# Where three turns of a weight conversion stand, and which scores go first, at the change from attention alone to attention beside dense products

## The chip, the cores and the metric

The kernel runs on one core of one Trainium2 chip. The metric is the device time of one execution in microseconds (us). Five engines work side by side, each through its own list of instructions in order: PE (matrix products; PEld is its weight load), DVE, ACT, POOL, and SP, which issues the DMAs.

## The reference

Attention with normalised queries and keys for 8 sequences, 12 heads, 448 positions, 64 wide, and then a SwiGLU block over the 8 x 448 = 3584 rows of 768. Inputs are float32, the three weight matrices arrive as float64.

```python
q_n, k_n = rmsnorm(q, g_q), rmsnorm(k, g_k)
scores = matmul(q_n, k_n^T) / sqrt(64)
attn = exp(scores - max) / (sum(exp(scores - max)) + 1e-9)
x = matmul(attn, v)                      # (8, 12, 448, 64) -> (3584, 768)
xn = x / sqrt(mean(x * x) + 1e-6) * rms_g
g, val = xn @ w_gate, xn @ w_val         # 768 -> 1536
out = (g * sigmoid(g) * val) @ w_out     # 1536 -> 768
```

## The kernel before

**Pairs of heads.** Attention is done two heads at a time: 48 pairs, six to a sequence, numbered g = 0 to 47. The main loop (L1276) has one block for each g. In block g the scores of pair g are made, pair g - 1 is finished, and pair g + 1 is transposed. The 448 key positions are three chunks of 128 and a remainder of 64, the "rest". The pieces of a block are these functions.

- `score(g, cs)`, L537: for each chunk in `cs` and both heads one product (L545) into a bank of `ps_s` (four banks), and an exponential on ACT (L549) into a tile `e`.
- `rests(g)`, L570: the rest's scores of pair g (L575, into a bank of `ps_s`); then, for pair g - 1, the first products of its output `av` (L581) and, for the first seven pairs, of its denominator `den` (L586); then the rest's exponential (L590). `av` lies in `ps_m`, a single bank, which is free again when pair g - 2's output has been read (L625).
- `values(g - 1)`, L592: the other products of `av` (L597). `sums(g - 1)`, L600: the other products of `den` (L610), the reciprocal on DVE (L614), and x = av * reciprocal on DVE (L625). Some steps later ACT squares x (L630) and POOL adds it to the sequence's sum of squares `ss` (L631).

**The bridge.** When a sequence's six pairs are done, `rms_x` (L640) sums `ss` over partitions by small products into `msx` (L645), DVE scales it (`ms`, L647), and POOL takes the power -1/2 (`rs`, L649). `norm_x` (L651) spreads `rs` over partitions by transposes into `rb` (L657), and six DVE instructions scale x by it (L663). Then the dense products can begin.

**The dense work** is cut into items that `fill` (L1155) puts between the pieces of the blocks. For sequence 0 they are, with numbers that are used below: items 0 to 47, gate and value products (L1122), item k using weight piece k; items 48 to 53, the first half of the output projection's columns for two row tiles of three parts each (L1004, four weight pieces of 48 to 59 each); items 54 to 59, the second half, with pieces 60 to 71. The first item comes in block 7, items 51 to 58 in block 13. From sequence 1 on, the weights are read back from DRAM, where the conversion stores them (`keep`, L772).

**The conversion** of the float64 weights to float32 is a pipeline in software. There are 72 pieces of 128 x 384, and `convert()` (L775) is one turn of it. Turn n issues the load of piece n on SP (L727), the *split* of piece n - 3 on ACT (two instructions, L740 and L741), the *join* of piece n - 4 on DVE (three, L746 to L748), the *add* of piece n - 5 on POOL (L785), and the store of piece n - 7 on SP (L773). There are 79 turns. The tile `top`, which a split writes and the add reads last, has four buffers (for some of the first 24 pieces three more of another pool). So the split of piece n waits for the add of piece n - 4.

Turns are issued at set places: 4 in block 0, 3 each in blocks 1 to 5, 3 at the end of block 6, which makes 22, and then one after every item. An item also carries the number of turns that must have been issued before it. Where that is not reached, `fill` issues the missing turns at once, one behind the other. For the output projection it is

```python
return [(NFC // OUT_PARTS * HALF, 4 * NFC + NFC * (n + 1) + 7, 0, ...)     # L1148
while turn_of["n"] < turns:                                                # L1166
    if not convert(): pe(idle)
pe(fn)
convert()
```

which gives 67 for items 48 to 53 and all 79 for items 54 to 59.

**Order.** Each engine's list follows the order in which the code issues. `pe(step)` counts one step on, runs it, and then runs what `after(n, ...)` has put n steps later.

Of the kernel before, what the change touches and what calls it, by code (L numbers as in the profile page):

```python
# [22 lines left out]
NPAIR = H // 2  # L23
# [312 lines left out]
def safe_scores(  # L336
# [42 lines left out]
    def after(n, fn):  # L379
        due.append((now["t"] + n, fn))  # L380

    def pe(fn):
        now["t"] += 1
        fn()
        for item in [d for d in due if d[0] <= now["t"]]:
            due.remove(item)
            item[1]()


    NG = B * NPAIR  # L390
# [4 lines left out]
    def own(j):  # L395
        return slice(j * D, (j + 1) * D)

    def across(j):
        return own(1 - j)
# [26 lines left out]
    def load_rests(b, i, engine):  # L426
        if b >= B:
            return
        if i == 0:
            st["rest", b] = rest_pool.tile([128, NPAIR, 2, D], F32, name="rest")  # L430
        for h in range(2):
            engine.dma_start(out=st["rest", b][own(i), :, 1 - h], in_=(q, k)[i][b, h::2, LAST].rearrange("h i d -> i h d"))

    def load_v_rests(b):
        if b >= B:
            return
        vr = st["vr", b] = rest_pool.tile([128, NPAIR, D], F32, name="vr")
        for h in range(2):
            nc.sync.dma_start(out=vr[across(h)], in_=v[b, h::2, LAST].rearrange("h i d -> i h d"))
# [31 lines left out]
    def direct(g):  # L471

        return g <= NPAIR
# [63 lines left out]
    def score(g, cs):  # L537

        qT, kT, rs = st["qT", g], st["kT", g], st["rs", g]
        sc = {}  # L540
        for c in cs:
            for j in range(2):
                r = across(j)
                ps = sc[c, j] = ps_s.tile([128, 512], F32, name="sc", tag="s")
                nc.tensor.matmul(ps[:, 0:S], lhsT=kT[r, c * 128:(c + 1) * 128], rhs=qT[r, :], start=True, stop=True)  # L545
        for (c, j), ps in sc.items():
            e = st["e", g, c, j] = e_pool.tile([128, S], F32, name="e")
            n = 2 * NK + c * 2 + 1 - j
            nc.scalar.activation(e, ps[:, 0:S], ACT.Exp, scale=rs[:, n:n + 1])  # L549


        def first():
            for j in range(2):
                es = st["es", g, j] = tmp.tile([128, S], F32, name="es", tag="es", bufs=4)
                nc.gpsimd.tensor_tensor(es, st["e", g, 0, j], st["e", g, 1, j], ALU.add)  # L555

        def more(of):
            for j in range(2):
                r = across(j) if of == "rest" else slice(0, 128)
                e = st["e", g, of] if of == "rest" else st["e", g, of, j]  # L560
                es = st["es", g, j]
                nc.gpsimd.tensor_tensor(es[r], es[r], e[r], ALU.add)  # L562

        if NK - 1 in cs and not direct(g):
            n = 3 if g == NPAIR + 1 else 2
            after(n, first)
            after(n + 2, lambda: more(2))
            after(n + 3, lambda: more("rest"))

    def rests(g):  # L570

        if g < NG:
            ps = ps_s.tile([128, 512], F32, name="sc", tag="s")
            for r in (own(0), own(1)):
                nc.tensor.matmul(ps[r, 0:S], lhsT=st["kT", g][r, LAST], rhs=st["qT", g][r, :], start=True, stop=True)  # L575
        if g:
            b, hp = divmod(g - 1, NPAIR)
            vr, e = st["vr", b][:, hp], st["e", g - 1, "rest"]
            av = st["av", g - 1] = ps_m.tile([128, 512], F32, name="av", tag="m")
            for j in range(2):  # L580
                nc.tensor.matmul(av[own(j), 0:S], lhsT=vr[across(j)], rhs=e[across(j)], start=True, stop=False,  # L581
                                 skip_group_check=True)
            if direct(g - 1):
                den = st["den", g - 1] = ps_f.tile([128, 512], F32, name="den", tag="f")
                for j in range(2):
                    nc.tensor.matmul(den[own(j), 0:S], lhsT=ones[across(j)], rhs=e[across(j)], start=True, stop=False,  # L586
                                     skip_group_check=True)
        if g < NG:
            e = st["e", g, "rest"] = e_pool.tile([128, S], F32, name="e")
            nc.scalar.activation(e, ps[:, 0:S], ACT.Exp)  # L590

    def values(g):  # L592

        vt, av = st["v", g], st["av", g]
        for c in range(NK):
            for j in range(2):
                nc.tensor.matmul(av[own(j), 0:S], lhsT=vt[:, j, c], rhs=st["e", g, c, j], start=False,  # L597
                                 stop=(c == NK - 1), skip_group_check=True)
# [41 lines left out]
    def rms_x(b):  # L640
        assert st["summed", b] == NPAIR - 1
        ss = st.pop(("ss", b))
        ps = (ps_s if b else ps_f).tile([128, 512], F32, name="msx", tag="s" if b else "f")
        for t in range(NT):
            nc.tensor.matmul(ps[0:P, t:t + 1], lhsT=ss[:, t * P:(t + 1) * P], rhs=ones[:, 0:1], start=True, stop=True)  # L645
        ms = small.tile([P, NT], F32, name="ms4")
        nc.vector.tensor_scalar(ms, ps[0:P, 0:NT], 1.0 / DM, 1e-6, ALU.mult, ALU.add)  # L647
        rs = st["rx", b] = small.tile([P, NT], F32, name="rs4")
        nc.gpsimd.tensor_tensor(rs, ms, mhalf[0:P, 0:NT], ALU.pow)  # L649
# [600 lines left out]
    def turns(n):  # L1250

        for _ in range(n):
            convert()
# [22 lines left out]
    for g in range(NG + 1):  # L1276
        b, hp = divmod(g, NPAIR)
        if g:
            load_pair(g + 3)
        if hp == 2:  # L1280
            for i in range(2):
                load_rests(b + 1, i, nc.sync)
            load_v_rests(b + 1)
        if g == 0:
            pe(lambda: score(0, (0,)))
            pe(lambda: rests(0))
            pe(lambda: score(0, (1,)))
            pe(lambda: turn(1, 0))
            pe(lambda: score(0, (2,)))
            norm_rests(0, 2, 4)  # L1290
            squares(2, 0)
            squares(2, 1)
            pe(lambda: turn(1, 1))
            for _ in range(3):
                convert()
            load_pair(3)
            load_v(2)
            convert()
            load_rows()
            continue  # L1300
        if g <= NPAIR:
            pe(lambda: score(g, (0,)))
            squares(g + 2, 0)
            squares(g + 2, 1)
            if g > 1:
                pe(lambda: turn(g + 1, 0))
                some_rests(g)
                pe(lambda: turn(g + 1, 1))
            pe(lambda: rests(g))
            pe(lambda: values(g - 1))  # L1310
            if g == 1:
                pe(lambda: turn(g + 1, 0))
                some_rests(g)
                pe(lambda: turn(g + 1, 1))
            load_v(g + 2)

            turns(1 if g == 1 else 3 if g < NPAIR else 0)
            pe(lambda: sums(g - 1))
            pe(lambda: score(g, (1, 2)))
            turns(2 if g == 1 else 3 if g == NPAIR else 0)  # L1320
            if g == 2:
                bound()
            continue

        pe(lambda: (rests(g), score(g, (0,)) if g < NG else None))
        if g == NPAIR + 1:
            pe(lambda: rms_x(0))
        pe(lambda: values(g - 1))
        load_v(g + 2)
        if g == NPAIR + 1:  # L1330
            pe(lambda: score(g, (1,)))
            pe(lambda: norm_x(0))
            pe(lambda: score(g, (2,)))
        pe(lambda: sums(g - 1))
        if g == NPAIR + 1:
            begin(0, 15)
        elif g < NG:
            pe(lambda: score(g, (1, 2)))
        st["block"] = now["t"]
        if hp:  # L1340
            fill()
            squares(g + 2, 0)
            squares(g + 2, 1)
            pe(lambda: turn(g + 1, 0))
            some_rests(g)
            fill()
            pe(lambda: turn(g + 1, 1))
            fill()
            continue
        fill(3)  # L1350
        pe(lambda: turn(g + 1, 0))
        fill(1)
        pe(lambda: rms_x(b - 1))
        squares(g + 2, 0)
        squares(g + 2, 1)
        pe(lambda: turn(g + 1, 1))
        fill(len(todo))
        begin(b - 1, 16)
        pe(lambda: norm_x(b - 1))
        fill()  # L1360
# [41 lines left out]
```

## Time and profile before

| | |
|---|---|
| median of 4 runs | 1597.73 us (1596.56 to 1598.63) |
| the profiled execution's own time | 1596.74 us |
| its span in the profile | 1595.0 us |
| PE busy | 1571.7 us, 99% |
| DVE busy | 872.3 us, 55% |
| ACT busy | 470.0 us, 29% |
| POOL busy | 658.7 us, 41% |

Times inside the execution count from the start of the span. The profiled execution's own time is its span and 1.74 us that lie around it. The shares of busy time are a mean over two unlike parts: up to about 280 us the weights are converted, and in most 20 us windows of that part DVE is busy for 15 to 19 us; afterwards DVE, ACT and POOL are busy about half of the time or less. PE is close to full in both.

### The profile page before, as it was taken

The page shows a single profiled execution, that of the slowest core. Times are in us where ns is not written, and L with a number is a line of the kernel's source. Part 1 is how long each engine was busy: PE and PEld are TensorE (multiplying, and loading weights), DVE is VectorE, ACT ScalarE, POOL GpSimd, SP SyncE. Part 2 cuts the span into 40 slices and gives each one's busy share as a digit, 9 for nine tenths or more (in the row PEclk, how much of TensorE's full clock was granted, in tenths as well). Part 3 has the DMA queues.
Part 4 walks back from the last instruction along what each step waited for, and adds up shares of the span by engine and source line. Part 5 has one row for each costly group of instructions (what it writes and reads, how often), then busy time and mean ns, then how long its engine had stood idle before and what let it go on. Part 6 is the DMA issues. An engine that isn't in the chain of part 4 may idle for free.

```text
span 1595.0 us, 21559 instructions
## 1 busy us (share of the span) xinstructions
PE 1571.7 (99%) x7286; PEld 1113.4 (70%) x7286; DVE 872.3 (55%) x1556; ACT 470.0 (29%) x940; POOL 658.7 (41%) x712
## 2 busy tenths in 40 slices
PE   8999999999999999999999999999999999999998
PEld 4344445687756887578865788667885688759974
DVE  6889898578822556236562354635563355613531
ACT  6746563232222222222232222323322222101010
POOL 6867877465334443344333443344542342000000
PEclk9999999999999999999999999999999999999999
DMA  7648574957746554465544655584554544457651
GB/s 210 206 151 257 162 251 124 289 187 243 250 141 204 156 154 121 141 205 155 154 119 142 205 154 148 149 266 132 160 146 124 176 141 139 120 176 214 174 154 52
DMA packets 261996, 273.28 MB, mean 171 GB/s; under 512 B 78836, under 2 KB 258804, under 8 KB 261876
## 3 DMA queue, kind: packets, MB, share of 16 engines
q1 hardware_dynamic: 260948, 271.61, 56.6%
q8 instruction: 60, 0.98, 0.3%
q14 instruction: 60, 0.49, 0.1%
q10 hardware_dynamic: 800, 0.20, 0.1%
q0 software_dynamic: 128, 0.00, 0.0%
HBM read 232.40 MB, written 39.32 MB: 170 GB/s over the span
## 4 chain that ended last, share of the span: by engine, by line
PE 78%; DVE 7%; issue 1%; DMA 0%; POOL 0%; SPq 0%; ACT 0%; DVEq 0%; POOLq 0%
PE ff L902 39%; PE ff L1094 22%; PE sc L545 6%; PE av L597 5%; PE sc L575 2%; PE den L610 2%; PE tr L527 1%; DVE top L747 1%; DVE top L748 1%; DVE top L746 1%; PE ff L1004 1%; DVE rd L618 1%; DVE h L925 0%; DVE h L924 0%; DVE ms L487 0%
## 5 line engine op out<-in xcount | busy, mean ns | idle before, releaser
L902 PE MATMUL ff<-x,w 128*128 128x224 f32 x1878 | 381.5, 354 | 0.1
L902 PEld LDWEIGHTS ff<-x,w 128*128 128x128 f32 x1878 | 351.3, 190 | 15.3 <-issue 11.7
L555 POOL TENSOR_TENSOR es<-e 128x448 f32<-128x448 f32 x82 | 91.5, 1137 | 493.0 <-ACT e L549 493.0
L902 PE MATMUL ff<-xs,w 128*128 128x224 f32 x1374 | 281.7, 353 | 4.5 <-DVE w L858 2.9
L902 PEld LDWEIGHTS ff<-xs,w 128*128 128x128 f32 x1374 | 258.0, 190 | 8.8 <-issue 6.0
L562 POOL TENSOR_TENSOR es<-es,e 64x448 f32<-64x448 f32 (+1 forms) x164 | 191.6, 1179 | 6.3
L618 DVE RECIPROCAL rd<-rd 128x448 f32<-128x448 f32 x41 | 121.0, 2952 | 113.5 <-ACT rd L617 113.5
L549 ACT ACTIVATE e<-sc,rs 128x448 f32<-128x448 f32 x288 | 161.2, 634 | 50.4 <-PE sc L545 48.0
L1094 PE MATMUL ff<-w,h 128*128 128x384 f32 x498 | 167.8, 487 | 0.6 <-ACT p L1073 0.6
L1094 PE MATMUL ff<-w,raw 128*128 128x384 f32 x468 | 159.6, 487 | 0.3 <-DVE y L1066 0.3
L545 PE MATMUL sc<-qT,kT 64*128 64x448 f32 x576 | 138.0, 572 | 1.9 <-ACT e L549 0.7
L1094 PEld LDWEIGHTS ff<-w,h 128*128 128x128 f32 x498 | 93.5, 190 | 64.5 <-issue 1.3
L1094 PEld LDWEIGHTS ff<-w,raw 128*128 128x128 f32 x468 | 87.6, 190 | 60.9 <-issue 2.6
L597 PE MATMUL av<-e,vt 128*64 128x448 f32 x576 | 118.8, 548 | 0.0
L506 POOL TENSOR_TENSOR rs<-ms,mhalf 128x12 f32<-128x12 f32 (+1 forms) x50 | 114.5, 2291 | 4.2
L1122 PE MATMUL ff<-x,w 128*128 128x448 f32 x288 | 111.8, 541 | 0.0
L545 PEld LDWEIGHTS sc<-qT,kT 64*128 64x128 f32 x576 | 53.9, 185 | 82.4 <-issue 68.5
L914 DVE TENSOR_TENSOR cc<-ff,u 128x448 f32<-128x448 f32 x84 | 52.3, 622 | 87.3 <-PE ff L902 87.2
L597 PEld LDWEIGHTS av<-e,vt 128*64 128x64 f32 x576 | 37.1, 136 | 75.6 <-issue 74.2
L1122 PEld LDWEIGHTS ff<-x,w 128*128 128x128 f32 x288 | 53.3, 190 | 50.8 <-issue 49.0
L631 POOL TENSOR_TENSOR ss<-ss,rd 128x448 f32<-128x448 f32 x40 | 46.5, 1163 | 82.9 <-ACT rd L630 82.9
L935 ACT COPY p<-ff 128x448 f32<-128x448 f32 x42 | 22.4, 532 | 192.6 <-PE ff L902 192.6
(132 smaller groups left out, 1858.3 us busy)
## 6 DMA issues: line engine op xcount, KB each, us to landing
w<-kept SPq DMA_DIRECT2D x511, 192.0 KB, 2.6
w<-kept_o SPq DMA_DIRECT2D x296, 192.0 KB, 2.8
kept<-w SPq DMA_DIRECT2D x89, 192.0 KB, 3.8
qk<-in_q_dram SPq DMA_DIRECT2D x48, 192.0 KB, 2.9
qk<-in_k_dram SPq DMA_DIRECT2D x96, 96.0 KB, 3.3
vt<-in_v_dram SPq DMA_DIRECT2D x48, 192.0 KB, 2.5
raw<-in_moe_w_gate_dram SPq DMA_DIRECT2D x24, 384.0 KB, 4.5
raw<-in_moe_w_val_dram SPq DMA_DIRECT2D x24, 384.0 KB, 4.6
```

The costliest lines, as they stand in the source:

```text
L506: nc.gpsimd.tensor_tensor(st["rs", g][:, cols], ms, mhalf[:, cols], ALU.pow)
L545: nc.tensor.matmul(ps[:, 0:S], lhsT=kT[r, c * 128:(c + 1) * 128], rhs=qT[r, :], start=True, stop=True)
L549: nc.scalar.activation(e, ps[:, 0:S], ACT.Exp, scale=rs[:, n:n + 1])
L555: nc.gpsimd.tensor_tensor(es, st["e", g, 0, j], st["e", g, 1, j], ALU.add)
L562: nc.gpsimd.tensor_tensor(es[r], es[r], e[r], ALU.add)
L597: nc.tensor.matmul(av[own(j), 0:S], lhsT=vt[:, j, c], rhs=st["e", g, c, j], start=False, stop=(c == NK - 1), skip_group_check=True)
L618: nc.vector.reciprocal(rd, rd)
L631: after(1 if soon else 4, lambda: (nc.gpsimd.tensor_tensor(ss, ss, rd, ALU.add), st.update({("summed", b): hp})))
L902: nc.tensor.matmul(bank[:, w * HT:(w + 1) * HT], lhsT=wt[:, c * 128:(c + 1) * 128], rhs=x[:, c, :], start=onto is None and w == c == 0, st ...
L914: nc.vector.tensor_tensor(add[name], ps[:, 0:S], add[other], ALU.add)
L1094: nc.tensor.matmul(ps, lhsT=left_o(b, which, LEFT_O[name], c), rhs=data(("wo", b, name, c)), start=first and c == 0, stop=c == NFP - 1, sk ...
L1122: nc.tensor.matmul(bank[w][:, 0:S], lhsT=data(key)[:, c * 128:(c + 1) * 128], rhs=st["x", 0, half][:, c, :], start=half == c == 0, stop=ha ...
```

## The change

In block 6, the last of the first sequence, the three turns of the conversion at the end of the block are left out; the count of 79 stays, so that they are issued later. In block 7 the scores of chunk 0 are issued ahead of `rests(7)`, and the two are separate steps of `pe`; before, `rests(7)` came first and both were one step. All other blocks go as they did.

```diff
             turns(1 if g == 1 else 3 if g < NPAIR else 0)
             pe(lambda: sums(g - 1))
             pe(lambda: score(g, (1, 2)))
-            turns(2 if g == 1 else 3 if g == NPAIR else 0)
+            turns(2 if g == 1 else 0)
             if g == 2:
                 bound()
             continue
 
-        pe(lambda: (rests(g), score(g, (0,)) if g < NG else None))
         if g == NPAIR + 1:
+            pe(lambda: score(g, (0,)))
+            pe(lambda: rests(g))
             pe(lambda: rms_x(0))
+        else:
+            pe(lambda: (rests(g), score(g, (0,)) if g < NG else None))
         pe(lambda: values(g - 1))
         load_v(g + 2)
         if g == NPAIR + 1:
```

## The prediction

> **What bounds the kernel now.** I read the page first, for the shares, then the waits of PE in the first 320 us, because block 7 and the whole conversion lie there, then the timeline at each wait, and last the chain of waits towards the place where the conversion ends.
>
> ```profile
> PE 1571.7 (99%) x7286; PEld 1113.4 (70%) x7286; DVE 872.3 (55%) x1556; ACT 470.0 (29%) x940; POOL 658.7 (41%) x712
> ```
>
> PE is idle for 23.3 us of the span. What the change can win is a part of that, and PE's waits name the part:
>
> ```profile
> PE av L581 <- issue: 1.2, 1, 1.2
> PE rb L657 <- POOL rs L649: 1.0, 1, 1.0
> ```
>
> Both lie between pair 6's last scores and the first dense product. PE's timeline, and DVE's below it:
>
> ```profile
> 83.82 0.97 PE L575 MATMUL sc<-qT,kT 64*64 64x448 f32 x4
> 85.98 0.97 PE L581 MATMUL av<-e,vr 64*64 64x448 f32 x4 [1.19 <-issue]
> 86.75 0.95 PE L586 MATMUL den<-e,ones 64*64 64x448 f32 x4
> 87.63 1.02 PE L545 MATMUL sc<-qT,kT 64*128 64x448 f32 x4
> 88.58 0.95 PE L645 MATMUL msx<-ones,ss 128*112 128x1 f32 x8
> 89.46 2.48 PE L597 MATMUL av<-e,vt 128*64 128x448 f32 x12
> 91.86 1.02 PE L545 MATMUL sc<-qT,kT 64*128 64x448 f32 x4
> 93.91 0.60 PE L657 MATMUL rb<-ident,rs 112*128 112x112 f32 x4 [1.02 <-POOL rs L649]
> ```
> ```profile
> 85.26 0.62 DVE L625 TENSOR_TENSOR x<-av,rd 128x448 f32<-128x448 f32 x1
> ...
> 92.13 0.56 DVE L748 SCALAR_TENSOR_TENSOR top<-raw,top 128x384 int32<-128x384 int32 x1
> 92.61 0.15 DVE L647 TENSOR_SCALAR ms<-msx 112x4 f32<-112x4 f32 x1
> ```
>
> The wait at 85.98 ends with pair 5's x (85.26 + 0.62 = 85.88), which frees the only `av` bank. The wait at 93.91 is the conversion's: `msx` is summed by 89.5, but `ms` stands on DVE behind three joins until 92.61, and `rs` and `rb` come after it. From 97.8 PE runs on the dense products. Where the conversion ends, the chain of waits runs through it:
>
> ```profile
> 272.49 0.93 DVE ms L487 x2
> ...
> 273.82 2.47 POOL rs L506
> ...
> 277.34 1.95 POOL w L785 x2
> 279.29 0.04 issue
> 279.34 3.82 PE ff L1004 x11
> ```
>
> The two adds are those of pieces 70 and 71. The products of 279.34 read piece 71, as the last pair of item 56. So the conversion arrives here just with PE: it has no room left at all.
>
> **The change, part by part.** All times are on the clock of before.
>
> *The scores first.* They take the place of the rests at 83.82 and fill the hole: two banks of `ps_s` come free with the exponentials that run from 83.13 at about 0.55 each. They take 0.95 (87.63 to 88.58), and the rests' 0.97 end at about 85.75. L581 still waits for x and starts at 85.98 as now; it and L586 take until 87.63. There `msx` is next, 0.95 earlier than now, if `ss` is ready. The square on ACT starts with x's end at 85.97 and takes 0.58; POOL's sum started at 86.63 and took 1.51, against 1.14 at 77.83. With no joins on DVE I take 1.14: ready at 87.8, `msx` at 87.85 instead of 88.58.
>
> *The turns gone from here.* Six ACT, nine DVE, three POOL instructions and three loads and three stores on SP leave. Behind them stood `ms` on DVE, `rs` on POOL, and on ACT and SP the rest's exponential and pair 10's loads, for which nobody waits. `ms` then follows `msx` at 88.9, `rs` takes 1.02 and is there at 90.1. PE has values and scores to do until 87.85 + (91.86 + 0.95 - 88.58) = 92.08, so `rb` starts at 92.08 without a wait, not at 93.91: **1.83 us won**. The six scalings (3.64) and the denominator behind `rb` keep their distances, so the dense items start 1.83 earlier, and so does the DVE work that waits for `rb`.
>
> *The turns come back.* After item k the turns issued are now 20 + k, not 23 + k. Items 0 to 47 need only piece k, for which 6 + k turns are enough (the code asks for 11 + k at most). Items 48 to 53 need 67, which 19 + 48 just reaches, and piece 59's add at item 45 (about 250 in the trace) is ahead of its use at about 256. Items 54 to 59 need 79: item 53 leaves 76 now and 73 after the change. So `fill` issues six turns in a row instead of three, in front of item 54. In those three of now only one add is left (piece 71); in the six there are four adds (68 to 71), three joins (69 to 71) and two splits (70, 71). The moved turns' three loads and stores spread over places where SP's loads come tens of us ahead; I cost them at nothing, and at some tenths if a load of a pair lands late.
>
> *What the burst costs.* On POOL the add after item 53 is at 277.30, behind pair 15's norm, whose place doesn't change; it is now piece 67's. The next adds follow about 0.97 apart (277.30 to 279.28 for two): 68 ready at 279.3, 69 at 280.3, 70 at 281.2. Piece 71 hangs on a longer thread: its split needs the `top` buffer that add 67 frees at 278.3; 0.56 on ACT gives 278.95; then its join on DVE. A join of now ends the DVE list in 1.33 alone and takes 2.96 beside adds:
>
> ```profile
> 224.21 0.57 DVE L746 TENSOR_SCALAR top<-top 128x384 f32<-128x384 f32 x1 [0.97 <-ACT top L740]
> 224.82 1.06 DVE L747 TENSOR_SCALAR top<-top 128x384 int32<-128x384 int32 x1
> 225.91 1.26 DVE L748 SCALAR_TENSOR_TENSOR top<-raw,top 128x384 int32<-128x384 int32 x1
> ```
> ```profile
> 222.26 4.50 POOL L785 TENSOR_TENSOR w<-top,raw 128x384 int32<-128x384 int32 x4
> ```
>
> It lies beside adds 68 to 70, so I take 2.96: joined at 281.95, added by 283.0. PE, which without waits would be at piece 67's use (item 55's last pair) at about 276.2 and at piece 71's at 279.1, stops at each piece in turn and reaches the last at 283.0 instead of 279.34: **3.66 us lost**. If the join took 1.33, the adds set the end at 282.2: 2.9 lost. If each of the five adds took 1.5 (the longest add in the trace took 1.507), they end at 284.8: 5.5 lost. Below 2.9 I find nothing: POOL has one add at a time.
>
> *Behind the burst.* The stores of the last pieces and the first weights of sequence 1 (279.67 on SP) stand behind the last add, and move with PE by the same amount, as do the differences on DVE that wait for those loads (284.49). The DVE waits of PE near 362 and 387 (1.4 and 1.5) follow the item order and stay.
>
> **The sum:** 1596.74 - 1.83 + 3.66 = 1598.6 for an execution like the profiled one. The median of the runs is 0.99 above it, so 1597.73 + 1.83 = **1599.6**. A measurement of this kernel can tell about 0.2%, 3.2 us, from no change.
>
> PE's clock matters where PE stops. The trace shows full clock (the 1.00 ahead of the DMA share) in the window that holds both waits of now:
>
> ```profile
> 80.00:100.00 20.00, 17.78 (x86) 6.96 (x83) 15.71 (x19) 10.16 (x20) 11.54 (x11) 1.00 0.69 213
> ```
>
> The longest single stop that I expect in the burst is 2.2 (276.2 to 278.4), twice the 1.19 that the trace shows at full clock, with other work on both sides; I take full clock.
>
> The Trainium skill (TensorE: Matmul & The Clock Gate, What's actually happening) says that an idle window of about 3.4 us halves PE's clock until a busy one of that length has passed. If the burst's stops did trip it, an estimate from that page adds 3.4 x (1 - 1/2) = 1.7 us and makes the sum 1601.3.
>
> **The rivals.** *The small loss* (the forecast): head won, burst lost, net 0 to +3.2. Own range 1597.8 to 1600.9. Chance 0.57.
>
> *The burst is free, or nearly:* only the head counts, 1595.9 with 1.83, down to 1594.9 if both waits go whole (1.19 + 1.02 on the profile's count, 2.8 with the modelled ends). For it: DVE was idle 2.20 before 277.32 and POOL 3.69 before 269.71, so the engines have time in sum. Against it: the adds stand behind pair 15's norm in POOL's list, and the idle time lies ahead of it. Faster by 3.2 would need the wait of 0.8 for `kT` near 241 to go as well. Chance 0.15, of which 0.06 is beyond 0.2%.
>
> *The burst costs more than 5.0:* PE's stop at item 56 grows past 3.2 + 1.83. One mechanism, the POOL adds in a row: it decides from about 1.4 us for each of five adds, which beside DVE joins some adds do take (1.33 to 1.5). At 1.5 the net is 5.5 - 1.83 = +3.7, 1601.4; if DVE's backlog (no wait of it from 225 to 275) also doesn't come 1.83 earlier, +5.5, 1603.2. Chance 0.28.
>
> *The change doesn't fill the hole at 85.98:* if pair 7's first scores wait for their banks, the first wait only changes its name, and the head wins 1.1 instead of 1.83. That shifts the forecast to 1600.3 and is inside it.
>
> **How the numbers follow.** Faster than 0.2%: 0.06. Slower than 0.2%: the third case, 0.28. The rest, 0.66, is within. The range leaves out the tail of the second case below 1595.5 and of the third above 1602.2.
>
> **What would show it.** In the changed profile: no wait before L581 above 0.3 and none before `rb`; the first L1122 at about 96.0; three adds (L785) fewer ahead of it; five adds in a row on POOL from about 275.5 to 281.2, with no other work of POOL between; PE waits on POOL L785 at L1004 of 3 to 4 us in sum, where PE had next to none before; from there all times 1.8 later than before. I am wrong if L1004 has no such wait, or if PE's new waits lie elsewhere.

## The result, and the profile after

Median 1600.77 us of 33 runs, against 1598.26 us of 53 runs of the kernel before. The ratio is 1.0015, 95% interval 1.0011 to 1.0020: some 2.4 us (1.8 to 3.2) slower, inside the 0.2% that a measurement of this kernel can tell from no change when it stands alone, and clear of zero with this many runs. The profiled execution took 1600.84 us, its span 1599.0 us.

Executions of all these kernels come in two groups about 1.6 us apart, which the first 12 us set; the profiled one of before is of the shorter group and that of after of the longer one, so below all steps are counted from pair 0's first scores (first L545, 10.81 before and 12.47 after). With this 1.66 taken off, the change shows two steps and nothing else:

| mark | before | after | difference, start taken off |
|---|---|---|---|
| first dense product (L1122) | 97.80 | 97.62 | -1.84 |
| first output product (L1004) | 248.77 | 248.57 | -1.86 |
| sequence 1's first product (L902) | 294.75 | 298.83 | +2.42 |
| end of the span | 1594.95 | 1599.05 | +2.44 |

**The head.** PE's timeline of after, from the rests to the first dense product, and DVE's beside it:

```profile
86.97 0.97 PE L575 MATMUL sc<-qT,kT 64*64 64x448 f32 x4
87.67 0.97 PE L581 MATMUL av<-e,vr 64*64 64x448 f32 x4
88.44 0.95 PE L586 MATMUL den<-e,ones 64*64 64x448 f32 x4
89.50 0.95 PE L645 MATMUL msx<-ones,ss 128*112 128x1 f32 x8
...
93.73 0.60 PE L657 MATMUL rb<-ident,rs 112*128 112x112 f32 x4
```
```profile
86.94 0.62 DVE L625 TENSOR_TENSOR x<-av,rd 128x448 f32<-128x448 f32 x1
90.48 0.16 DVE L647 TENSOR_SCALAR ms<-msx 112x4 f32<-112x4 f32 x1 [2.92 <-PE msx L645]
94.37 3.05 DVE L663 SCALAR_TENSOR_TENSOR x<-x,rg,rb 128x448 f32<-128x448 f32 x5 [3.72 <-PE rb L657]
```

Neither L581 nor L657 has a wait in brackets any more. DVE now waits 2.92 us for `msx`, where before the finished `msx` waited for DVE, and then 3.72 us for `rb`.

**The burst.** PE's waits between 262 and 300 us (there were none in this stretch before), POOL's and ACT's timeline there, and two windows of 5 us, in which the figure ahead of the DMA share is the granted clock:

```profile
PE ff L1004 <- POOL w L785: 2.6, 1, 2.6
```
```profile
276.13 1.26 POOL L511 TENSOR_TENSOR qn<-qk,rs 128x192 f32<-128x192 f32 x2
277.35 4.46 POOL L785 TENSOR_TENSOR w<-top,raw 128x384 int32<-128x384 int32 x4
282.36 1.00 POOL L785 TENSOR_TENSOR w<-top,raw 128x384 int32<-128x384 int32 x1 [0.55 <-issue]
```
```profile
278.70 0.55 ACT L740 ACTIVATE top<-raw 128x384 f32<-128x384 f32 x1 [6.71 <-POOL w L785]
```
```profile
275.00:280.00 5.00, 2.39 (x10) 1.32 (x9) 3.35 (x8) 1.03 (x2) 4.92 (x6) 1.00 0.33 117
280.00:285.00 5.00, 5.00 (x11) 2.18 (x10) 2.66 (x3) 0.48 (x1) 4.29 (x5) 0.66 0.49 169
```

Five adds stand in a row behind pair 15's norm, and the last split waits for the add of piece 67, as the prediction had it. What it had not: the granted clock falls to half from 280.0 to 283.4. This hardly costs anything here. Item 56's four weight pieces are taken up by PE at 279.80, 280.86, 282.22 and 283.48, and the adds that they need end at 279.65, 280.73, 281.81 and 283.36. The third piece is taken up 0.4 us behind its add, because products at half clock follow 0.64 us apart. The last is taken up 0.12 behind its add, just when the slow products ahead of it are through. So two limits end within 0.1 us of each other, the row of adds and the slow products, and the clock costs that 0.1 at most.

### The profile page after: what moved, and what is told of

The parts are those of the page before. It is cut to its first block, busy times and chain, and to the rows that moved or that the text cites. A ratio compares the mean times of both kernels' runs of the same rounds, so it can differ in the third digit from the quotient of the medians.

```text
span 1599.0 us, 21562 instructions
## 1 busy us (share of the span) xinstructions
PE 1575.5 (99%) x7286; PEld 1115.7 (70%) x7286; DVE 870.9 (54%) x1556; ACT 470.7 (29%) x940; POOL 660.2 (41%) x712
## 4 chain that ended last, share of the span: by engine, by line
PE 81%; DVE 6%; issue 0%; DMA 0%; POOL 0%; ACT 0%; DVEq 0%
PE ff L902 40%; PE ff L1094 22%; PE sc L545 6%; PE av L597 5%; PE sc L575 2%; PE den L610 2%; PE ff L1004 2%; PE tr L527 1%; DVE top L747 1%; DVE top L748 1%; DVE top L746 0%; PE ff L1122 0%; DVE h L925 0%; DVE h L924 0%; DVE rd L618 0%
## 5 line engine op out<-in xcount | busy, mean ns | idle before, releaser
L902 PE MATMUL ff<-x,w 128*128 128x224 f32 x1878 | 381.5, 354 | 0.1
L902 PEld LDWEIGHTS ff<-x,w 128*128 128x128 f32 x1878 | 351.3, 190 | 15.3 <-issue 11.1
L902 PE MATMUL ff<-xs,w 128*128 128x224 f32 x1374 | 281.7, 353 | 4.4 <-DVE w L858 2.9
L902 PEld LDWEIGHTS ff<-xs,w 128*128 128x128 f32 x1374 | 258.0, 190 | 8.6 <-issue 6.0
L545 PE MATMUL sc<-qT,kT 64*128 64x448 f32 x576 | 138.5, 572 | 1.9 <-ACT e L549 0.7
L545 PEld LDWEIGHTS sc<-qT,kT 64*128 64x128 f32 x576 | 54.2, 185 | 82.6 <-issue 69.2
L1122 PE MATMUL ff<-x,w 128*128 128x448 f32 x288 | 111.8, 541 | 0.0
L1122 PEld LDWEIGHTS ff<-x,w 128*128 128x128 f32 x288 | 53.3, 190 | 50.8 <-issue 49.0
L785 POOL TENSOR_TENSOR w<-top,raw 128x384 int32<-128x384 int32 x63 | 67.8, 1088 | 34.9 <-DVE top L748 25.7
L631 POOL TENSOR_TENSOR ss<-ss,rd 128x448 f32<-128x448 f32 x40 | 46.4, 1160 | 82.4 <-ACT rd L630 82.4
```

Of the source, the lines that this page charges most:

```text
L785: nc.gpsimd.tensor_tensor(data(key).bitcast(I32), top, lo, ALU.add)
L902: nc.tensor.matmul(bank[:, w * HT:(w + 1) * HT], lhsT=wt[:, c * 128:(c + 1) * 128], rhs=x[:, c, :], start=onto is None and w == c == 0, st ...
L1122: nc.tensor.matmul(bank[w][:, 0:S], lhsT=data(key)[:, c * 128:(c + 1) * 128], rhs=st["x", 0, half][:, c, :], start=half == c == 0, stop=ha ...
```

## The experiments

Twelve kernels that differ from before or after in a few words. The table gives what each did by its profile, in us against before with the start taken off, and the measured ratio to the kernel before. The stretches are bounded by the marks of the table above.

| run | to first dense product | to first output product | to sequence 1 | behind it | span | ratio (95% interval) |
|---|---|---|---|---|---|---|
| the change | -1.84 | -0.02 | +4.28 | +0.02 | +2.44 | 1.0015 (1.0011 to 1.0020) |
| e1, turns only | -1.03 | -0.01 | +4.31 | +0.08 | +3.35 | 1.0022 (1.0013 to 1.0032) |
| e2, order only | +0.03 | +0.04 | -0.01 | -0.17 | -0.10 | 1.0 (0.9991 to 1.0009) |
| e3, given back in block 7 | -1.83 | +6.43 | +0.02 | -0.17 | +4.45 | 1.0032 (1.0019 to 1.0044) |
| e4, norm later on POOL | -1.86 | -0.03 | +6.11 | +0.20 | +4.42 | 1.0022 (1.0013 to 1.0031) |
| e5, one turn kept | -1.43 | +0.01 | +2.46 | -0.07 | +0.98 | 1.0006 (0.9997 to 1.0015) |
| e6, two mid, one end | -1.46 | +0.06 | 0.00 | +0.01 | -1.40 | 0.9992 (0.9983 to 1.0001) |
| e7, three mid | -1.34 | +0.06 | 0.00 | +0.05 | -1.23 | 0.9992 (0.9983 to 1.0001) |
| e8, free top buffer | -1.81 | +0.04 | +4.30 | +0.08 | +2.61 | 1.0016 (1.0007 to 1.0025) |
| e9, three behind `ms` | -1.62 | +2.10 | -0.01 | -0.26 | +0.21 | 1.0003 (0.9994 to 1.0012) |
| e10, two mid, one behind `ms` | -1.85 | +0.02 | +0.01 | -0.10 | -1.91 | 0.9987 (0.9978 to 0.9996) |
| e11, two mid, one end, old order | -1.08 | +0.02 | -0.02 | -0.04 | -1.11 | 0.9995 (0.9986 to 1.0004) |
| e12, e4 with PE kept busy | -1.80 | +0.03 | +3.51 | +0.22 | +1.95 | 1.0012 (1.0003 to 1.0021) |

### The two halves of the change

e1 takes the turns out and keeps the old order:

```diff
-            turns(2 if g == 1 else 3 if g == NPAIR else 0)
+            turns(2 if g == 1 else 0)
```

> Only the three turns leave block 6; the rests stay ahead of the scores. My theory: the wait of av (L581) near 86 stays, the wait of rb (L657) goes, so the first dense product comes 1.1 us earlier than before; the burst in front of item 54 is that of the full change and costs 4.3 us. Sum +3.2 us against before, 0.8 us above the full change. Rival (the turns alone win the whole head): first dense product 1.85 us earlier, sum +2.4 us.

It did what the theory said: -1.03 and +4.31, sum +3.35. PE's wait for `av` is there as before:

```profile
88.01 0.97 PE L581 MATMUL av<-e,vr 64*64 64x448 f32 x4 [1.20 <-issue]
```

e2 is the change with `3 if g == NPAIR` put back in that line, so that only the order differs.

> Only the order of the first scores and the rests of pair 7 is changed; the three turns stay in block 6. My theory: the hole before av (L581) is filled, but ms (L647) still stands on DVE behind three joins, which end at 92.6 us whatever PE does, so rb (L657) starts at 93.9 as before and the wait of 1.0 us before it grows to about 1.7: 0 us against before, and no burst. Rival (each part is worth its own wait): first dense product 0.75 us earlier, sum -0.75 us.

The hole before `av` is gone and nothing is won; the time went into a wait of 0.49 us of `msx` for the sum of squares on POOL and into a longer wait for `rb` (1.41, before 1.02), since `ms` still stands on DVE behind the joins until 92.69:

```profile
94.00 0.60 PE L657 MATMUL rb<-ident,rs 112*128 112x112 f32 x4 [1.41 <-POOL rs L649]
```
```profile
92.22 0.56 DVE L748 SCALAR_TENSOR_TENSOR top<-raw,top 128x384 int32<-128x384 int32 x1
92.69 0.15 DVE L647 TENSOR_SCALAR ms<-msx 112x4 f32<-112x4 f32 x1
```

So the order alone is worth 0, the turns alone 1.03, both together 1.84. The burst belongs to the turns alone.

### Is it the missing three turns, and where else can they stand?

e3 gives the turns back in block 7, one behind each of its three groups of items (`fill()`), so that item 54 finds 76 turns as before.

```diff
+            more = 1 if g == NPAIR + 1 else 0
             fill()
+            turns(more)
             squares(g + 2, 0)
 ...
             fill()
+            turns(more)
             pe(lambda: turn(g + 1, 1))
             fill()
+            turns(more)
             continue
```

> The full change, and the three missing turns are issued in block 7, one after each of its three groups of dense items, so that 76 turns are out after item 53 again and the burst is three turns long as before. My theory (the loss is the longer burst alone): the head keeps its 1.85 us and the wait of L1004 on the add is back at 0.1 us: -1.85 us against before, 4.2 us below the full change. Rival (the conversion has no room between 98 and 277 us, so 60 turns there instead of 57 push its whole chain back): the adds of pieces 70 and 71 come 2 to 4 us later than before relative to PE and the sum is between 0 and +2 us.

The burst is gone (+0.02), which shows that it was the missing turns. But 6.43 us were lost at a new place, more than the rival had allowed, and not where the rival put it: between 105 and 130 us, not at the adds of pieces 70 and 71. PE's and ACT's waits and a window of that run:

```profile
PE sc L545 <- ACT e L590: 3.5, 1, 3.5
```
```profile
ACT top L740 <- DMA raw<-in_moe_w_gate_dram: 7.2, 1, 7.2
```
```profile
125.00:130.00 5.00, 4.08 (x9) 2.17 (x10) 4.90 (x6) 4.43 (x9) 3.10 (x4) 0.66 1.08 358
```

A split waits 7.2 us on ACT for its weight piece, and pair 8's exponentials stand behind it in ACT's list; PE stops 3.5 us for their banks, and then the granted clock is half for 3.4 us: the eight score products behind the stop took 3.79 us, against 1.77 for eight of the kind in the kernel before (L545 near 82). What held the load is not shown.

e9 puts all three behind `ms`, in the 3.7 us in which DVE waits for `rb`. The others put turns in the middle of block 6, ahead of `sums(5)`: e7 all three, e6 two with the third at the end of the block, e10 two with the third behind `ms`. e11 is e6 with the old order of scores and rests. The edits in short:

```diff
 # e9: turns(3); e10: turns(1)
             pe(lambda: rms_x(0))
+            turns(3)
 # middle of block 6: e6, e10, e11 two; e7 three
-            turns(1 if g == 1 else 3 if g < NPAIR else 0)
+            turns(1 if g == 1 else 3 if g < NPAIR else 2)
 # end of block 6: e6, e11 one
-            turns(2 if g == 1 else 0)
+            turns(2 if g == 1 else 1 if g == NPAIR else 0)
```

> The full change, with the three turns issued in block 7 right behind the step that makes msx, ms and rs, so that their joins stand behind ms on DVE instead of in front of it, where DVE waits 3.7 us for rb. No longer burst (22 turns before item 0). My theory: rb as early as in the full change (-1.8 us); three joins need 4.0 us alone, up to 6 beside adds, so the scalings of x start 0.3 to 2.3 us later than rb allows, of which PE has 2.6 us of other work to hide it; sum -1.4 to -1.85 us against before. Rival (DVE's list from 98 to 277 us has no room, so its later start comes back at the adds of pieces 70 and 71): L1004 waits 0.4 to 2.3 us on the adds near 277, sum -1.4 to +0.5 us.

The head was as expected (-1.62) and 2.10 us were lost later, but again earlier than the rival had it: PE waits 1.8 us for a copy of `kT` on DVE near 112 (two waits of the kind up to 320 us; before had one, of 0.8).

```profile
PE tr L527 <- DVE kT L533: 2.7, 2, 1.8
```

The joins ran beside POOL's `rs` and adds and took 6.6 us, the scalings began at 97.24 instead of 94.37, and DVE did not make it up in 12 us.

> The full change, and the three turns go back into block 6: two in its middle, ahead of the sums of pair 5, where DVE idles 3.3 us ahead of the reciprocal, and one at its end. 22 turns are out before item 0 as before, so no longer burst. My theory (the slots ahead of rb were the only free DVE time, so the turns must stay ahead of it, but not in front of ms): the joins end before the reciprocal (82.3), ms follows msx at once, head -1.5 to -1.85 us, burst 0: sum -1.5 to -1.85 us against before. Rival (turns in the middle hold an exponential on ACT or the reciprocal on DVE): the wait of av near 86 comes back with 1 to 2 us, sum 0 us or above.

> The same with all three turns in the middle of block 6. My theory: three joins need 4.0 us where DVE idles 3.3, the reciprocal comes 0.7 us late, and av (L581) waits about 0.85 us: sum -1.2 us against before. Rival as for two in the middle: sum 0 us or above.

By the profile they win 1.40 and 1.23 us: e7 as the theory said, e6 0.1 less than its range. The ratios agree, but their intervals end just above 1. The heads fall 0.4 to 0.5 us short of the change's. In e7 the reciprocal and with it `av` start 0.5 us later than in the change. In e6 the join at the end of block 6 stands beside the sum of squares on POOL, and `msx` waits for it; that sum (L631) takes 1.50 us there, and 1.13 in the change, where no join is beside it.

```profile
88.23 0.95 PE L645 MATMUL msx<-ones,ss 128*112 128x1 f32 x8 [0.48 <-POOL ss L631]
```

> Two turns in the middle of block 6 and one at its end, but the rests of pair 7 stay ahead of its first scores. My theory: the wait of av near 86 stays, ms is free, and rb comes 1.05 us earlier than before: sum -1.05 us, so that the order is worth 0.4 us more once the turns are out of the way (in the run with the order alone it was worth nothing). Rival (the order is worth nothing in any place of the turns): -1.47 us.

-1.08: with the turns out of the way the order is worth 0.38 us, as expected.

> The full change, with two of the three turns in the middle of block 6 and the third right behind the step of msx, ms and rs. My theory: no join stands beside the sum of squares on POOL or ahead of ms, so the head is the full change's -1.85 us and not the -1.47 us of two in the middle and one at the end of block 6; the one join behind ms ends 2 us before rb; burst as before: -1.85 us against before. Rival (a turn in block 7 holds ACT's exponentials as it did where three were given back): PE waits on an exponential in block 7, sum -1 us or above.

-1.85 in the head and nothing lost behind it. The one join behind `ms` took 2.7 us beside POOL's `rs` and an add, and still left DVE 1.08 us to wait for `rb`:

```profile
94.61 3.64 DVE L663 SCALAR_TENSOR_TENSOR x<-x,rg,rb 128x448 f32<-128x448 f32 x6 [1.08 <-PE rb L657]
```

This version is faster than both kernels: 0.9987 of before (0.9978 to 0.9996), some 2.1 us, and 0.9972 of after by the two ratios. Against before that too is inside 0.2%. Three turns that cost 4.3 us as a burst cost nothing where DVE has time that ends in a wait for PE.

### What sets the length of the burst

e5 keeps one of the three turns at the end of block 6 (`1 if g == NPAIR`), so that the burst has five.

> The full change with one of the three turns left at the end of block 6, so that the burst in front of item 54 is five turns. If the loss there is adds in a row behind pair 15's norm, with piece 71 held by its top buffer only when that buffer is freed by an add of the same row (which needs six turns), then the row is four adds (4.5 us from 277.4) and piece 71 is ready 1.5 us earlier than in the full change: loss 2.7 instead of 4.3 us. The head keeps 1.5 to 1.85 us (one join is done before ms needs DVE). Sum +1.0 us against before (+0.8 to +1.2). Rival (each moved turn costs the same): loss 2.9 us and a head of 1.2, sum +1.6 us.

+2.46 in place of 4.28, with four adds in the row and no split waiting for one of them; sum +0.98. The head, -1.43, is just short of its range.

```profile
277.89 4.21 POOL L785 TENSOR_TENSOR w<-top,raw 128x384 int32<-128x384 int32 x4
```

The clock stays at 1.00 in the profiled execution, with a single stop of 1.6 us. This fits the row of adds (2.7 expected); a cost equal for each turn (2.9) is 0.4 off, so the two are not far apart.

e8 gives the last split a buffer that is free:

```diff
+        elif n == len(pieces) - 1:
+            top = raw_pool.tile([128, 2 * BW], I32, name="raw")[:, 0:BW]
```

> The full change, with the last piece's top in a buffer of the raw pool that is free by then, so that its split needn't wait for the add of piece 67. If that thread (split at 278.7, join until 282.2, add from 282.4) sets the end of the burst, the last join comes ahead and the last add follows the other four at once: piece 71 is ready 0.5 to 1 us earlier, sum +1.4 to +1.9 us against before. Rival (joins and adds get in each other's way on SBUF, so the row ends at the same time whatever the buffer): no change, sum +2.4 us.

No change (+4.30). The last add did come at the end of the row at once, but the row itself grew from 4.46 to 4.77 us for four adds, with the last join now beside them, and the last add ended only 0.2 us earlier:

```profile
277.56 4.77 POOL L787 TENSOR_TENSOR w<-top,raw 128x384 int32<-128x384 int32 x4
282.29 0.99 POOL L787 TENSOR_TENSOR w<-raw 128x384 int32<-128x384 int32 x1
```

PE could not use even that. The clock is at half here too, from 280.0 to 283.4, and the products in front of piece 71 let PE take it up at 283.72, 0.43 behind its add. By these two times, an estimate, full clock would have saved it 0.4 us. So the thread through the `top` buffer is worth 0.2 us of the adds' time, not the 0.5 to 1 of the theory.

e4 issues POOL's part of pair 15's norm behind the burst:

```diff
-            after(2, lambda: rms_qk(g))
-            after(2, lambda: norm_q(g))
+            late = 5 if g == 2 * NPAIR + 3 else 2
+            after(late, lambda: rms_qk(g))
+            after(late, lambda: norm_q(g))
```

> The full change, and POOL's part of the norm of pair 15 (ms, rs, qn; L505 to L511, 4 us) is issued three steps later, behind the six turns in front of item 54 instead of ahead of them. My theory (the burst's cost is the place of the adds in POOL's list, behind that norm): the add of piece 67 starts at about 273 instead of 277.3 on the clock of the full change, the others follow their joins (DVE reaches them at 275 to 279), and the last is done near 280, against 283.4: PE loses 0.2 to 1 us instead of 4.3, sum -1.0 to -1.7 us against before. Rival (DVE's joins and ACT's splits set the end, not POOL's order): the last add stays after 282, sum +1.5 us or more.

My theory failed: +6.11 in the profiled execution, worse than the change. The row of adds starts 4.3 us earlier, but then joins and adds alternate (each line number is one higher in this kernel). POOL and DVE:

```profile
275.75 1.00 POOL L786 TENSOR_TENSOR w<-top,raw 128x384 int32<-128x384 int32 x1 [1.03 <-DMA kept_o<-w]
277.78 1.00 POOL L786 TENSOR_TENSOR w<-top,raw 128x384 int32<-128x384 int32 x1 [1.03 <-PE ff L1005]
```
```profile
275.83 1.13 DVE L748 TENSOR_SCALAR top<-top 128x384 int32<-128x384 int32 x1
277.00 0.56 DVE L749 SCALAR_TENSOR_TENSOR top<-raw,top 128x384 int32<-128x384 int32 x1
277.48 0.35 DVE L747 TENSOR_SCALAR top<-top 128x384 f32<-128x384 f32 x1
277.86 1.14 DVE L748 TENSOR_SCALAR top<-top 128x384 int32<-128x384 int32 x1
```

The join's second instruction, 0.36 us alone, ends 0.2 us behind the add that runs beside it, and the next add begins only when the join is through: 2.03 us for each piece. The last add still ended 0.8 us earlier than in the change (280.8, against 283.4 less 1.7 for the start). What made the run slower was the clock. PE's stops at item 56, and the window behind them:

```profile
276.80 0.91 PE L1005 MATMUL ff<-w,h 128*128 128x384 f32 x2 [0.83 <-POOL w L786]
278.83 1.17 PE L1005 MATMUL ff<-w,h 128*128 128x384 f32 x2 [1.12 <-POOL w L786]
280.87 8.69 PE L1005 MATMUL ff<-w,h 128*128 128x384 f32 x18 [0.87 <-POOL w L786]
```

```profile
280.00:285.00 5.00, 4.13 (x8) 2.31 (x8) 0.06 (x1) 0.48 (x1) 4.68 (x5) 0.50 0.64 193
```

It was half from 279.4 to 286.2, and from 280.9 on beside no wait. The drop did not come in every execution of e4: the three quickest took 1598.8 to 1598.9 us at a mean clock of 0.999, the two slowest 1603.1 and 1603.3 at 0.996. e12 tests this. It is e4 with small products, which compute nothing that is used, in the stops of item 56 (`spare` is a bank of `ps_s`, given for this item alone):

```diff
         for fc in range(part * each, (part + 1) * each):
+            for _ in range(3 if spare is not None and fc > part * each else 0):
+                nc.tensor.matmul(spare[:, 0:128], lhsT=ident, rhs=ident, start=True, stop=True)
             nc.tensor.matmul(ps, lhsT=st["h", b, fc][:, i * 128:(i + 1) * 128], ...)
```

> The run with pair 15's norm behind the six turns, and in item 56 three products of 128x128 into a spare bank ahead of each of the last three weight pieces, about 0.8 us of TensorE work into each stop of 1.3 us or more. In the run without them the last add was done 0.8 us earlier than in the full change, but the granted clock fell to 0.5 from 279.4 to 286.2 us, and the 9 products behind piece 71 took 0.65 us each instead of 0.32. My theory (the three stops of about 1 us, with PE busy for under 40% of 3.4 us, halve the clock, and this alone made that run no better): the clock stays at 1.00, the products behind piece 71 go at 0.32 us, and the loss between the first output product and sequence 1's first product is 3.5 us instead of 6.1; sum +1.6 us against before. Rival (the slow products have another cause, such as the adds and joins on SBUF): the loss stays at 6 us or grows by the added products, sum +4.4 us or more.

+3.51, where the theory said 3.5, and the clock is 1.00 throughout; the whole span, at +1.95, is 0.3 above the theory's sum:

```profile
280.00:285.00 5.00, 4.54 (x19) 2.85 (x18) 0.52 (x2) 0.48 (x1) 4.41 (x5) 1.00 0.66 191
```

Its executions took 1598.7 to 1599.0 and 1600.3 to 1600.6 us, with none of the long ones of e4, and the quickest of e4 took as long as the quickest of e12. So the norm's place in POOL's list does count, by 0.8 us of the 4.28. The rest is left to the adds and joins themselves; how it divides between them no run shows.

## Why the prediction was right

**The time.** Forecast +1.83 against before, measured +2.4 (1.8 to 3.2): sign and place hold, 0.6 short. Of the 1.2 us between the forecast 1599.6 and the median of 1600.77, the other 0.5 is the median of before, 1597.73 of 4 runs and 1598.26 of 53.

**The head** was forecast at -1.83 and is -1.84. The split of it that the prediction implied holds too: e1 and e2 show that the filled hole is worth nothing as long as `ms` stands behind the joins.

**The burst** was forecast at 3.66 and is 4.28, and this is the term that was mis-sized. The row was right (five adds behind pair 15's norm, the last split held by the add of piece 67), and so was the thread behind that split: its join took 2.94, forecast 2.96. But the split came about 0.5 us late on the forecast's clock: `qn` took 1.26 instead of 0.97 and the add of piece 67 took 1.31 instead of 1.0, both beside the join of piece 70. I had put the slowing on the joins only. Some 0.1 more is the clock. e8 shows that mending the thread alone hardly helps, since the row of adds is nearly as long.

**Below 2.9 I find nothing** was right for this burst, and **costed at nothing** for the moved loads and stores: no load of a pair is late in the change (-0.02 up to the first output product).

**The clock** was the step that failed. I took full clock through the burst, because the longest stop expected was 2.2 us. The stop at piece 67 was 2.6 and the clock was half for 3.4 us. By the sum alone this would have been 1.7 us, the figure that the prediction worked out from the Trainium skill (TensorE: Matmul & The Clock Gate, What's actually happening) and left out. It cost 0.1 us at most, since PE had to wait for the adds of these 3.4 us anyway. That was luck: the sum left the term out for a reason that did not hold, and with adds done 0.2 us earlier, as in e8, the slow products already set PE's time. In e3 and in most of e4's drop there was no wait beside it, and it was paid for: e12, which takes the drop away, loses 2.6 us less than e4.

**What would show it:** the two waits gone, 15 adds in place of 18 ahead of the first dense product, that product (97.62 less 1.66 is 95.96, forecast 96.0) and five adds in a row came as described. The waits of 3 to 4 us in sum didn't: the profile books 2.6, and the rest is hidden in products at half clock that it counts as busy.

**The rivals.** The third (adds of 1.4 us and more) was not reached: the five took 1.0 to 1.3. The second, the burst for nothing, is what e10 makes of the kernel, but by taking the burst away. The fourth, a hole that stays, did not come: L581 starts without a wait.

## What to carry to other kernels

Work that waits for nothing, such as a conversion, is cheapest where the engine that does it would idle for another reason; before such work is taken out of a gap, find the next place where its pipeline is late; here it came back there. On engines with lists in order, a step costs what stands behind it: three turns cost 0 or 6.4 us within 30 us of this kernel, by what stood behind them on ACT and DVE. And of two waits in a row, ending the first alone can be worth nothing: here 0, the second alone 1.03, both together 1.84.

## What the runs showed of the hardware

**The clock can fall without one long stop.** A single stop of 1.8 us in full work left the clock at 1.00 (e9), and so did one of 1.6 (e5); stops of 2.6 us (after) and 3.5 us (e3) halved it for 3.4 us. In e4 it fell at 279.4, behind stops of 0.83 and 1.12 us with two products between them, and stayed at half for two stretches of 3.4 us; with small products in the same stops it did not fall (e12). The page named above speaks of an idle window; here PE was at work for 1.4 of the 3.4 us ahead of the drop (0.91 from 276.80 and 0.53 from 278.83, in e4). That fits a measure of how busy PE was over some stretch. Where its limit lies no run shows, nor why the drop came in some executions of e4 only.

**The first products can run at half clock, and the whole kernel moves by it.** The second ten of the products that only warm PE up, in before and in after:

```profile
7.25 1.28 PE L1241 MATMUL warm<-ident 128*128 128x128 f32 x10
```
```profile
7.55 2.34 PE L1241 MATMUL warm<-ident 128*128 128x128 f32 x10
```

The same ten products take nearly twice the time, and the first scores come 1.66 us later. In after the trace has no record of the clock ahead of 10.4 us (in before, none ahead of 5.2), so half clock is inferred there from the doubled time. In e10, which starts as late (12.71), the profile shows it, in the window from 8 to 10 us:

```profile
8.00:10.00 2.00, 2.00 (x12) 2.00 (x11) 1.74 (x6) 0.54 (x2) 1.83 (x3) 0.50 0.91 241
```

Both kinds of start were seen with kernels that are the same up to there, so a comparison of two single runs of this kernel can be off by 1.6 us, two thirds of what this change does.

**A DVE instruction can wait for a POOL one to end.** The join's second instruction (L747) takes 0.36 us alone, and 1.04 to 1.17 beside an add of 1.0; in 13 of the 21 cases in before it ends 0.22 us behind the add, as in e4's lines above. The add is slowed less, from 1.00 to mostly 1.12 to 1.15, at most 1.34, beside a join. That the one waits for the other fits these times; what they share no run shows.
